# An FFT filter and gated FFN on one core: three of eight batches pass from first to second stage through DRAM, and the second stage runs two iterations later

## The chip, the cores and the metric

The kernel runs on one core of a Trainium2 chip. The metric is the device time of one execution in microseconds, as the median of a few runs. A profiled execution has a span of its own, from its first to its last instruction. The engines of the core are TensorE (PE in the profile; PEld is its weight load), VectorE (DVE), ScalarE (ACT), GpSimd (POOL) and SyncE (SP), which here only issues copies.

## The reference

The input `x` has 8 batches of 3136 rows and 256 columns. Along the rows it is filtered by multiplication in the frequency domain; the result goes through a gated feed-forward block of width 1024.

```python
X = np.fft.rfft(x, axis=1)
y = np.fft.irfft(X * (filt_r + 1j * filt_i)[None], n=3136, axis=1)   # (8, 3136, 256)
h = np.maximum(y @ w_in, 0.0)                                        # (8, 3136, 1024)
conv_out = sum(conv_w[k] * hp[:, k:k + S, :] for k in range(3))      # hp: h padded by one row at each end
out = (h * sigmoid(conv_out)) @ w_out                                # (8, 3136, 256)
```

## The kernel before

**The transform.** 3136 is 112 x 28, and both transforms are done as two small matrix products each. For one batch there are four stages: the first stage (112-point, over `n1`), the second stage (28-point, over `n2`), the product with the filter, the third stage (back over `n2`) and the last stage (back over `n1`). Between the first and the second stage the data has to change places: the first stage has one column block per `n2`, with the 112 rows of (part r, group g) on one axis, and the second stage wants the rows of (n2, r), again 112, for one group g. A batch is cut into 14 pairs p (`NP = 14`), two `n2` in the first stage, two groups in the later ones.

- `first(b, p)` holds the loaded piece of `x` as weights and streams the table `s1_sb` through, so its result comes out with the 256 columns of `x` on the partitions (two blocks of 128). `keep` (L327) copies it with ACT into one of two big tiles `turns[0]`, `turns[1]`, used alternately by batch.
- `turn(b, p)` (L334) transposes four blocks of a finished `turns` tile back with PE against the identity `eye_sb`, which brings the rows (n2, r) of two groups onto the partitions. `turned_rows` (L339) copies that with ACT into a tile named `a` (two buffers).
- `second(b, p)` (L346; L349 for the last pair) multiplies it with `s2_sb` into the PSUM tile `pp` (three buffers).
- `filt(b, p)` makes three products on DVE (L358, L359, L360) and one sum `z` on POOL (L362).
- `third(b, p)` (L233) multiplies `z` with `i1_sb`; `store` (L237, L239) copies the result with ACT and ACT's queue writes it to DRAM as `b_dram`.
- `last_load`, `last_stage` (L215) and `last_out` (L146, L149) read it back and make `y`.

**The order of the first loop.** It is written out by hand: one iteration i handles the pair i-1 in the first stage and, with m = i - SKEW and SKEW = NP + 1 = 15, the pair m in `turn`, m-1 in `second`, m-2 in `filt` and m-4 in `third`; a whole batch must have passed the first stage before its first pair can be turned. On PE the order inside an iteration is third, first, second, turn. The engines PE, ACT, DVE and POOL keep this order; SP's copies are placed by their dependences. `load_first` loads `x` six iterations ahead of its use, into seven buffers; from iteration 10 on `load_filter` brings the filter and the third stage's table, a pair per iteration; from iteration 36 on one step (two in every eighth iteration) of `convert_weights` unpacks the FFN's weights with DVE, ACT and POOL. The steps last until about iteration 106. At iteration `done` = 113 the pools of `x` and the raw weights are closed and `y` gets their place; from then on batch 0 passes the last stage in the place of the first.

**The second loop** runs over 448-row tiles and 128-column blocks of the FFN: `inner` (L177 to L179), `relu`, `conv`, `gate`, `split_g` and `project` (L498 to L500). The last stage of batches 1 to 7 is spread over it.

Of the kernel before, what the change touches and what calls it, by code (L numbers as in the profile page):

```python
# [9 lines left out]
F32 = mybir.dt.float32  # L10
# [3 lines left out]
AF = mybir.ActivationFunctionType  # L14
# [4 lines left out]
N2 = 28  # L19
G = 28  # L20
D = 256
# [103 lines left out]
def tile_fft_filter_gated_ffn(  # L125
# [16 lines left out]
    nc = tc.nc  # L142
    B = x.shape[0]
# [35 lines left out]
        nc.tensor.matmul(ps, lhsT=wl, rhs=rh, start=False, stop=stop, **kw)  # L179

    dram = ctx.enter_context(tc.tile_pool(name="dram", bufs=1, space=bass.MemoryType.DRAM))
    b_dram = [dram.tile([N2, 112, D], F32, name=f"b_dram{b}") for b in range(B)]

    wc = ctx.enter_context(tc.tile_pool(name="wc", bufs=1))
# [24 lines left out]
    def last_stage(b, c, ps):  # L209

        br = lasts[b, c]
        for j in range(2):
            for k in range(KT):
                o = ps[:, (2 * k + j) * N1:(2 * k + j + 1) * N1]
                nc.tensor.matmul(o, lhsT=br[:, j, 128 * k:128 * k + 128], rhs=m2_sb, start=True, stop=True)  # L215
        lasts[b, c] = ps

    def last_out(b, c):
        yh, yl = y_slices(b, slice(c, c + 2))
        pv = lasts.pop((b, c))[:, 0:4 * N1].rearrange("p (k c a) -> p k c a", c=2, a=N1)  # L220
        hi_act(yh, pv)
        lo_dve(yl, pv, yh)

    NP = 14
# [5 lines left out]
    def third(b, p, ps):  # L230
        z = parts.pop((b, p))
        for j in range(2):
            nc.tensor.matmul(ps[:, j], lhsT=i1_sb[:, 2 * p + j], rhs=z[:, j], start=True, stop=True)  # L233

    def store(b, p, ps):
        st = rest.tile([112, 2, D], F32, name="sb")
        nc.scalar.activation(st, ps, AF.Copy)  # L237
        v = b_dram[b].rearrange("n (r g) d -> (n r) g d", g=G)
        nc.scalar.dma_start(out=v[:, 2 * p:2 * p + 2], in_=st)  # L239
# [4 lines left out]
    s1_sb = xp.tile([112, N2, 112], F32, name="s1_sb")  # L244
    with (
# [5 lines left out]
        turns = [pl.tile([128, KT, N2, 112], F32, name=f"turn{k}") for k, pl in enumerate((xp, fc))]  # L251
# [9 lines left out]
        nc.gpsimd.memset(t1_sb[32:64], 0.0)  # L261

        rows = {}

        def load_filter(p):

            sl = slice(2 * p, 2 * p + 2)
            nc.sync.dma_start(out=t2_sb[0:56, sl], in_=fi[0:56, sl])
            nc.sync.dma_start(out=t1_sb[64:120, sl], in_=fr[64:120, sl])
            if p == NP - 1:  # L270
                nc.sync.dma_start(out=t1_sb[0:56, sl], in_=fr[0:56, sl])
            nc.sync.dma_start(out=i1_sb[:, sl], in_=i1[:, sl])
# [44 lines left out]
        def first(b, p):  # L317

            r = rows.pop(("x", b, p))
            ps = fps.tile([128, 512], F32, name="ps")[:, 0:448].rearrange("p (k n m) -> p k n m", k=KT, n=2)  # L320
            for j in range(2):
                for k in range(KT):
                    nc.tensor.matmul(ps[:, k, j], lhsT=r[:, j, 128 * k:128 * k + 128], rhs=s1_sb[:, 2 * p + j], start=True, stop=True)  # L323
            return ps

        def keep(b, p, ps):
            nc.scalar.activation(turns[b % 2][:, :, 2 * p:2 * p + 2], ps, AF.Copy)  # L327

        def turn(b, p):
            ps = fps.tile([112, 2, D], F32, name="ps")  # L330
            for j in range(2):
                for k in range(KT):
                    v = turns[b % 2][:, k].rearrange("p n (r g) -> p (n r) g", g=G)[:, :, 2 * p + j]
                    nc.tensor.transpose(ps[:, j, 128 * k:128 * k + 128], v, eye_sb)  # L334
            return ps

        def turned_rows(b, p, ps):
            r = fp.tile([112, 2, D], F32, name="a", bufs=2)
            nc.scalar.activation(r, ps, AF.Copy)  # L339
            rows["a", b, p] = r  # L340

        def second(b, p):
            r = rows.pop(("a", b, p))
            pp = fps.tile([120, 2, D], F32, name="pp", bufs=3)
            if p < NP - 1:
                nc.tensor.matmul(pp, lhsT=s2_sb, rhs=r, start=True, stop=True)  # L346
            else:
                for j, m in ((0, s2_sb), (1, s2s_sb)):
                    nc.tensor.matmul(pp[:, j], lhsT=m, rhs=r[:, j], start=True, stop=True)  # L349
            psums[b, p] = pp  # L350

        def filt(b, p):


            pp, v = psums.pop((b, p)), turned[p % 2]
            sl = slice(2 * p, 2 * p + 2)
            u = fp.tile([120, 2, D], F32, name="u")
            nc.vector.tensor_mul(u, pp, t1_sb[:, sl])  # L358
            nc.vector.tensor_mul(v[64:120], pp[0:56], t2_sb[0:56, sl])  # L359
            nc.vector.tensor_mul(v[0:56], pp[64:120], t2_sb[64:120, sl])  # L360
            z = rest.tile([120, 2, D], F32, name="z")
            nc.gpsimd.tensor_tensor(out=z, in0=u, in1=v, op=ALU.add)  # L362
            parts[b, p] = z

        def at(i):
            return divmod(i, NP) if 0 <= i < NP * B else None

        XBUFS = 7
        SKEW = NP + 1

        def load_first(i):
            if i < NP and i % 2 == 0:
                nc.sync.dma_start(out=s1_sb[:, 2 * i:2 * i + 4], in_=s1[:, 2 * i:2 * i + 4])
            if bp := at(i):
                load(*bp)
# [2 lines left out]
            load_first(i)  # L378
        csteps, wsteps = convert_conv(), convert_weights()
        done = NP * B + 1  # L380
        NI = done + N2 // 2 + 2
        END = NP * B - 4
        with tc.manual_schedule(engines=COMPUTE):
            for i in range(NI):
                m = i - SKEW
                if i == done:
                    assert next(wsteps, None) is None
                    convert_pools.close()
                    forward_pools.close()
                    yps.append(ctx.enter_context(tc.tile_pool(name="y_even", bufs=1, side="right", reuse_waits="tile")))  # L390
                    lp = ctx.enter_context(tc.tile_pool(name="lp", bufs=2, side="right", reuse_waits="tile"))
                if i:
                    load_first(i + XBUFS - 1)
                if i == 8:
                    nc.sync.dma_start(out=eye_sb, in_=eye)
                    nc.sync.dma_start(out=s2_sb, in_=s2[:, 0:120])
                    raws["cw"] = cv.tile([128, 6 * NF], I32, name="rawc", bufs=1)
                    nc.sync.dma_start(out=raws["cw"], in_=conv_w)
                if 10 <= i < 10 + NP:
                    load_filter(i - 10)  # L400
                if i == 16:
                    nc.sync.dma_start(out=s2s_sb, in_=s2s[:, 0:120])
                    nc.sync.dma_start(out=m2_sb, in_=m2)
                c = 2 * (i - done)
                if 0 <= c - 4 < N2:
                    last_out(0, c - 4)
                if 0 <= c - 2 < N2:
                    last_stage(0, c - 2, fps.tile([128, 512], F32, name="ps"))
                if bp := at(m - 2):
                    filt(*bp)  # L410
                pt = None
                if (bp := at(m - 4)) and m - 4 <= END:
                    pt = fps.tile([112, 2, D], F32, name="ps")
                    third(*bp, pt)
                pf = first(*bp) if (bp := at(i - 1)) else None
                if bp := at(m - 1):
                    second(*bp)
                pa = turn(*bp) if (bp := at(m)) else None
                if pt is not None:
                    store(*at(m - 4), pt)  # L420
                if pf is not None:
                    keep(*at(i - 1), pf)
                if pa is not None:
                    turned_rows(*at(m), pa)
                if 0 <= m - 1 < NP:
                    copy_filter(m - 1)
                if 14 <= i < 22:
                    next(csteps, None)
                if i in (30, 32):
                    load_weights((i - 30) // 2)  # L430
                if i >= 36:
                    for _ in range(2 if i % 8 == 0 else 1):
                        next(wsteps, None)
                if 0 <= c < N2:
                    last_load(0, c)
# [14 lines left out]
    def projected(m):  # L450

        return None if m in PAUSE else at(m - PLAG + sum(m < k for k in PAUSE))

# [67 lines left out]
    for b in range(1, B):  # L521
        start = ((NSUB * (b - 1) - 1) // 2 + 1) * 16 + (4 if b == 1 else 0)
        stop = NSUB * b // 2 * 16 + NSUB * b % 2
# [3 lines left out]
    with tc.manual_schedule(engines=COMPUTE):  # L527
        for m in range(NH + PLAG):
            if m + 4 in pieces:
# [22 lines left out]
                evacuate(*a)  # L552


PLAG = 6
PAUSE = (8,)
AVOID = (3, 4, 5, 6, 7)
# [39 lines left out]
```

## Time and profile before

| | us |
|---|---|
| median of 3 runs (1558.48 to 1562.84) | 1561.46 |
| the profiled execution | 1559.94 |
| its span | 1558.2 |
| PE busy | 1537.8 (99%) |
| DVE busy | 1297.0 (83%) |
| ACT busy | 1245.0 (80%) |
| POOL busy | 703.0 (45%) |
| granted TensorE clock, mean | 0.999 |

The first loop takes about 364 us, the second the rest. In a row of the timeline, the first number is the start in us from the span's start, the second how long it lasts, then engine, line, operation, what is written and read (without buffer numbers), the shape and how many instructions were merged; a bracket gives the idle time just before and what ended it. In a row of a group, the time behind the bar is all of it together, then the mean of one in ns. A line number is one of the kernel before. A matmul in full precision shows as two records, since it passes twice.

### The profile page before, as it was taken

The numbers are of one execution on the slowest core, as the hardware profiler recorded it, in microseconds if no ns is written. First come the engines' busy times: TensorE is split into PE (matmuls) and PEld (weight loads), VectorE is DVE, ScalarE is ACT, GpSimd is POOL, SyncE is SP. The second block draws the span as 40 slices with busy tenths as digits, with TensorE's granted clock in tenths as the row PEclk, the third lists the DMA queues.
The fourth block names the chain that finished last, engine by engine and source line by source line (L and its number), as shares of the span: only waits on it lengthen the run. The fifth ranks groups of instructions, "written<-read, shape, count | busy, mean of one in ns | idle before, by whom it ended". The sixth has DMA issues, their size and how long they took to land.

```text
span 1558.2 us, 27801 instructions
## 1 busy us (share of the span) xinstructions
PE 1537.8 (99%) x10320; PEld 1418.2 (91%) x10320; DVE 1297.0 (83%) x1978; ACT 1245.0 (80%) x2274; POOL 703.0 (45%) x625
## 2 busy tenths in 40 slices
PE   8999999998999999999999999999999999999998
PEld 7787778877999999999999999999999999999998
DVE  3888888788888888888888888888888888888887
ACT  5655555566888888888888888888888888888887
POOL 3455555533444444444444444444444434444444
PEclk9999999999999999999999999999999999999999
DMA  9855555452111011111111011111011110100001
GB/s 236 261 179 168 172 169 164 137 148 78 33 52 48 31 47 48 49 49 47 48 42 36 27 53 52 44 48 48 31 48 42 49 54 27 46 25 25 24 25 48
DMA packets 89062, 115.24 MB, mean 74 GB/s; under 512 B 7400, under 2 KB 60168, under 8 KB 88928
## 3 DMA queue, kind: packets, MB, share of 16 engines
q1 hardware_dynamic: 74592, 87.77, 18.4%
q10 hardware_dynamic: 14336, 25.70, 5.8%
q8 instruction: 82, 1.34, 0.4%
q14 instruction: 52, 0.43, 0.1%
HBM read 62.06 MB, written 51.38 MB: 73 GB/s over the span
## 4 chain that ended last, share of the span: by engine, by line
PE 94%; DMA 2%; DVE 1%; ACT 1%; issue 0%; SPq 0%; POOL 0%; ACTq 0%; POOLq 0%; DVEq 0%
PE ps_h L178 12%; PE ps_h L179 12%; PE ps_h L177 11%; PE po L498 11%; PE po L500 11%; PE po L499 11%; PE ps L233 6%; PE ps_h L215 5%; PE pp L346 5%; PE ps L323 5%; PE ps L334 3%; DMA x<-in_x 1%; PE ps L215 1%; DVE y L149 1%; ACT y L146 0%; PE pp L349 0%
## 5 line engine op out<-in xcount | busy, mean ns | idle before, releaser
L152 POOL TENSOR_TENSOR g<-t,g 128x448 fp32r<-128x448 f32 x448 | 517.1, 1154 | 663.5 <-ACT g L146 259.3
L498 PE MATMUL po<-wo,g 128*128 128x256 f32 x1568 | 441.4, 282 | 0.0
L500 PE MATMUL po<-wo,g 128*128 128x256 f32 x1568 | 433.9, 277 | 0.4 <-POOL g L152 0.4
L499 PE MATMUL po<-wo,g 128*128 128x256 f32 x1568 | 433.4, 276 | 0.0
L472 DVE SCALAR_TENSOR_TENSOR t<-ps_h,cw,t 128x448 f32<-128x448 f32 x448 | 305.7, 682 | 85.6 <-ACT t L467 75.2
L178 PE MATMUL ps_h<-y,wi 128*128 128x450 f32 x896 | 330.3, 369 | 5.6 <-DVE y L149 5.6
L177 PE MATMUL ps_h<-y,wi 128*128 128x450 f32 x896 | 329.1, 367 | 3.3 <-DVE t L478 1.9
L179 PE MATMUL ps_h<-y,wi 128*128 128x450 f32 x896 | 328.8, 367 | 0.0
L473 DVE SCALAR_TENSOR_TENSOR t<-ps_h,cw,t 128x448 f32<-128x448 f32 x448 | 306.5, 684 | 16.0
L467 ACT ACTIVATE t<-ps_h,cw 128x448 f32<-128x448 f32 x448 | 284.8, 636 | 43.2 <-ACT ps_h L465 2.6
L498 PEld LDWEIGHTS po<-wo,g 128*128 128x128 f32 x1568 | 294.8, 188 | 7.1
L499 PEld LDWEIGHTS po<-wo,g 128*128 128x128 f32 x1568 | 294.3, 188 | 5.7
L500 PEld LDWEIGHTS po<-wo,g 128*128 128x128 f32 x1568 | 294.5, 188 | 0.6 <-POOL g L152 0.6
L465 ACT ACTIVATE ps_h<-ps_h 128x450 f32<-128x450 f32 x448 | 251.8, 562 | 32.9 <-PE ps_h L179 27.0
L478 DVE TENSOR_TENSOR t<-ps_h,t 128x448 f32<-128x448 f32 x448 | 275.3, 615 | 0.1
L477 ACT ACTIVATE t<-t 128x448 f32<-128x448 f32 x448 | 255.0, 569 | 12.4 <-DVE t L473 11.2
L146 ACT ACTIVATE g<-t 128x448 fp32r<-128x448 f32 x448 | 254.7, 568 | 0.2 <-DVE t L478 0.2
L362 POOL TENSOR_TENSOR z<-u,v 120x512 f32<-120x512 f32 x112 | 156.6, 1398 | 184.3 <-DVE v L360 154.1
L178 PEld LDWEIGHTS ps_h<-y,wi 128*128 128x128 f32 x896 | 168.3, 188 | 14.7 <-DVE y L149 7.9
L179 PEld LDWEIGHTS ps_h<-y,wi 128*128 128x128 f32 x896 | 168.3, 188 | 13.9
L177 PEld LDWEIGHTS ps_h<-y,wi 128*128 128x128 f32 x896 | 169.9, 190 | 11.7 <-DVE t L478 2.9
L149 DVE TENSOR_TENSOR y<-ps_h,y 128x448 fp32r<-128x448 f32 x98 | 103.1, 1053 | 75.3 <-ACT y L146 75.3
(62 smaller groups left out, 1661.6 us busy)
## 6 DMA issues: line engine op xcount, KB each, us to landing
x<-in_x SPq DMA_DIRECT2D x112, 224.0 KB, 2.9
b_dram<-sb ACTq DMA_DIRECT2D x112, 224.0 KB, 2.3
br<-b_dram SPq DMA_DIRECT2D x112, 224.0 KB, 2.6
out<-ot SPq DMA_DIRECT2D x27, 896.0 KB, 4.1
raw<-in_w_in SPq DMA_DIRECT2D x8, 256.0 KB
raw<-in_w_out SPq DMA_DIRECT2D x8, 256.0 KB
t_sb<-in_fr SPq DMA_DIRECT2D x15, 112.0 KB
t_sb<-in_fi SPq DMA_DIRECT2D x14, 112.0 KB
```

The costliest lines, as they stand in the source:

```text
L152: nc.gpsimd.tensor_tensor(out=dst, in0=src, in1=hi.bitcast(F32), op=ALU.subtract)
L177: nc.tensor.matmul(ps, lhsT=wh, rhs=rh, start=start, stop=False, **kw)
L178: nc.tensor.matmul(ps, lhsT=wh, rhs=rl, start=False, stop=False, **kw)
L179: nc.tensor.matmul(ps, lhsT=wl, rhs=rh, start=False, stop=stop, **kw)
L467: nc.scalar.activation(t, h[:, 1:SUB + 1], AF.Copy, scale=cw[:, 1, f:f + 1])
L472: nc.vector.scalar_tensor_tensor(out=t, in0=h[:, 0:SUB], scalar=cw[:, 0, f:f + 1], in1=t, op0=ALU.mult, op1=ALU.add)
L473: nc.vector.scalar_tensor_tensor(out=t, in0=h[:, 2:SUB + 2], scalar=cw[:, 2, f:f + 1], in1=t, op0=ALU.mult, op1=ALU.add)
L477: nc.scalar.activation(t, t, AF.Sigmoid)
L478: nc.vector.tensor_mul(t, h[:, 1:SUB + 1], t)
L498: nc.tensor.matmul(o, lhsT=gh[:, sl], rhs=wo[0][:, f], start=first, stop=False, skip_group_check=True)
L499: nc.tensor.matmul(o, lhsT=gh[:, sl], rhs=wo[1][:, f], start=False, stop=False, skip_group_check=True)
L500: nc.tensor.matmul(o, lhsT=gl[:, sl], rhs=wo[0][:, f], start=False, stop=last, skip_group_check=True)
```

## The change

Batches 2, 4 and 6 (`THROUGH_DRAM`) take another way from the first to the second stage. Their first stage holds the table `s1_sb` as weights and streams the piece of `x` through (two matmuls of 256 columns in place of four of 112), so its result has (r, g) on the partitions. `keep` copies it into a tile `a` and ACT's queue writes it to a new DRAM tensor `a_dram[b]`. `load_rows` reads two groups of it back with 112 rows (n2, r) on the partitions, on SP's queue, two iterations ahead of the place where `turn` would stand; `second` takes the tile as it is. For these batches there is no `turn`, no `turned_rows` and no `turns` tile; the two tiles alternate over batches 0, 1, 3, 5 and 7. The pool of `a` has four buffers, shared by `keep`, `load_rows` and `turned_rows`. SKEW goes from 15 to 17, so that all stages from the turn on are two iterations later, and so are `load_filter` and the last stage of batch 0 (`LATE` = 2).

```diff
+    a_dram = {b: dram.tile([N2, 112, D], F32, name=f"a_dram{b}") for b in THROUGH_DRAM}
...
+        turned_by = {b: n + 1 for n, b in enumerate(b for b in range(B) if b not in THROUGH_DRAM)}
...
         def first(b, p):
             r = rows.pop(("x", b, p))
+            if b in THROUGH_DRAM:
+                ps = fps.tile([112, 2, D], F32, name="ps")
+                for j in range(2):
+                    nc.tensor.matmul(ps[:, j], lhsT=s1_sb[:, 2 * p + j], rhs=r[:, j], start=True, stop=True)
+                return ps
...
         def keep(b, p, ps):
-            nc.scalar.activation(turns[b % 2][:, :, 2 * p:2 * p + 2], ps, AF.Copy)
+            if b in THROUGH_DRAM:
+                r = fp.tile([112, 2, D], F32, name="a", bufs=ABUFS)
+                nc.scalar.activation(r, ps, AF.Copy)
+                nc.scalar.dma_start(out=a_dram[b][2 * p:2 * p + 2].rearrange("n p d -> p n d"), in_=r)
+            else:
+                nc.scalar.activation(turns[turned_by[b] % 2][:, :, 2 * p:2 * p + 2], ps, AF.Copy)
+
+        def load_rows(b, p):
+            r = fp.tile([112, 2, D], F32, name="a", bufs=ABUFS)
+            v = a_dram[b].rearrange("n (r g) d -> (n r) g d", g=G)
+            nc.sync.dma_start(out=r, in_=v[:, 2 * p:2 * p + 2])
+            rows["a", b, p] = r
...
         def turned_rows(b, p, ps):
-            r = fp.tile([112, 2, D], F32, name="a", bufs=2)
+            r = fp.tile([112, 2, D], F32, name="a", bufs=ABUFS)
...
-        SKEW = NP + 1
+        ABUFS = 4
+        SKEW = NP + 3
+        LATE = SKEW - NP - 1
...
-        NI = done + N2 // 2 + 2
+        NI = done + LATE + N2 // 2 + 2
...
-                if 10 <= i < 10 + NP:
-                    load_filter(i - 10)
+                if 12 <= i < 12 + NP:
+                    load_filter(i - 12)
+                if (bp := at(m + 2)) and bp[0] in THROUGH_DRAM:
+                    load_rows(*bp)
...
-                c = 2 * (i - done)
+                c = 2 * (i - done - LATE)
...
-                pa = turn(*bp) if (bp := at(m)) else None
+                pa = turn(*bp) if (bp := at(m)) and bp[0] not in THROUGH_DRAM else None
...
+THROUGH_DRAM = (2, 4, 6)
```

On PE, where batch 1 ends its second stage and batch 2 begins, there stood before (L233 third stage, L323 first stage, L346 and L349 second stage, L334 turn):

```order
L346 MATMUL pp<-a,s_sb 120x512
L334 MATMUL ps<-eye_sb,turn_98 112x128 x4
L233 MATMUL ps<-z,i_sb 112x256 x2
L323 MATMUL ps<-s_sb,x 128x112 x4
L349 MATMUL pp<-a,s_sb 120x256
L349 MATMUL pp<-a,s2s_sb 120x256
L334 MATMUL ps<-eye_sb,turn_97 112x128 x4
L233 MATMUL ps<-z,i_sb 112x256 x2
L323 MATMUL ps<-s_sb,x 128x112 x4
L346 MATMUL pp<-a,s_sb 120x512
L334 MATMUL ps<-eye_sb,turn_97 112x128 x4
L233 MATMUL ps<-z,i_sb 112x256 x2
```

Each iteration has its four pieces, the turn among them. The same place after (L234 third stage, L330 first stage with `x` as weights, L364 and L367 second stage, L352 turn):

```order
L364 MATMUL pp<-a,s_sb 120x512
L352 MATMUL ps<-eye_sb,turn_100 112x128 x4
L234 MATMUL ps<-z,i_sb 112x256 x2
L330 MATMUL ps<-s_sb,x 128x112 x4
L367 MATMUL pp<-a,s_sb 120x256
L367 MATMUL pp<-a,s2s_sb 120x256
L234 MATMUL ps<-z,i_sb 112x256 x2
L330 MATMUL ps<-s_sb,x 128x112 x4
L364 MATMUL pp<-a,s_sb 120x512
L234 MATMUL ps<-z,i_sb 112x256 x2
L330 MATMUL ps<-s_sb,x 128x112 x4
```

The turn is gone from the iterations that carry batch 2 to the second stage; the order of the others is what it was. On SP, the copies around the first reads of batch 2, before (L314 loads `x`, L285 the raw weights):

```order
L285 DMA raw<-in_w_in 128x512
L285 DMA raw<-in_w_out 128x512
L314 DMA x<-in_x 112x512 x9
L285 DMA raw<-in_w_in 128x512
L285 DMA raw<-in_w_out 128x512
L314 DMA x<-in_x 112x512 x9
```

And after (L316 loads `x`, L287 the raw weights, L344 reads the rows of batch 2 back):

```order
L287 DMA raw<-in_w_in 128x512
L287 DMA raw<-in_w_out 128x512
L316 DMA x<-in_x 112x512 x2
L344 DMA a<-a_dram_57 112x512 x2
L316 DMA x<-in_x 112x512
L344 DMA a<-a_dram_57 112x512
L316 DMA x<-in_x 112x512
L344 DMA a<-a_dram_57 112x512
L316 DMA x<-in_x 112x512
```

The two first reads follow one another; after them each read stands behind one load of `x`, and loads of `x` stand behind reads.

More of the change, by code (lines that the diff above doesn't have):

```diff
@@ L332, in turn @@
                 for k in range(KT):
-                    v = turns[b % 2][:, k].rearrange("p n (r g) -> p (n r) g", g=G)[:, :, 2 * p + j]
+                    v = turns[turned_by[b] % 2][:, k].rearrange("p n (r g) -> p (n r) g", g=G)[:, :, 2 * p + j]
                     nc.tensor.transpose(ps[:, j, 128 * k:128 * k + 128], v, eye_sb)
```

## The prediction

> **What bounds the kernel now.** I read the busy shares first, then the chain of waits, then the busy time by stretches, then TensorE's own timeline. The first line is part 1 of the page, the second its chain.
>
> ```profile
> PE 1537.8 (99%) x10320; PEld 1418.2 (91%) x10320; DVE 1297.0 (83%) x1978; ACT 1245.0 (80%) x2274; POOL 703.0 (45%) x625
> ```
> ```profile
> PE 94%; DMA 2%; DVE 1%; ACT 1%; issue 0%; SPq 0%; POOL 0%; ACTq 0%; POOLq 0%; DVEq 0%
> ```
>
> TensorE (PE) is the bound on average, but a share of 99% can hide a stage with another limit. So the next view cuts the span: columns are the stretch, its length, then busy us (and count) of PE, PEld, DVE, ACT, POOL, the granted clock, the DMA share and GB/s.
>
> ```profile
> 0.00:20.00 20.00, 14.99 (x106) 14.58 (x107) 0.00 (x0) 8.01 (x14) 7.29 (x8) 1.00 0.92 262
> ...
> 100.00:140.00 40.00, 40.00 (x239) 31.95 (x238) 33.81 (x50) 23.92 (x44) 22.88 (x19) 1.00 0.58 174
> ...
> 260.00:300.00 40.00, 40.00 (x238) 31.80 (x238) 32.63 (x50) 23.47 (x43) 23.22 (x17) 1.00 0.50 151
> ```
> ```profile
> 700.00:1500.00 800.00, 797.08 (x5547) 765.65 (x5546) 682.41 (x1055) 694.77 (x1284) 351.12 (x321) 1.00 0.13 41
> ```
>
> From about 60 to 350 us, where the change works, PE has no idle time at all; the start waits for loads; the second loop (from 365 us) is also full, so what the first loop saves reaches the end one for one. This is one steady iteration of the first loop on PE, with the start of each piece:
>
> ```profile
> 297.87 1.03 PE L233 MATMUL ps<-z,i_sb 120*112 120x256 f32 x4
> 298.73 1.04 PE L323 MATMUL ps<-s_sb,x 112*128 112x112 f32 x8
> 299.61 1.03 PE L346 MATMUL pp<-a,s_sb 112*120 112x512 f32 x2
> 300.48 0.60 PE L334 MATMUL ps<-eye_sb,turn 128*112 128x128 f32 x4
> 300.92 1.03 PE L233 MATMUL ps<-z,i_sb 120*112 120x256 f32 x4
> ```
>
> Matmuls overlap, so the second column is no price; the distance between starts is: third stage 0.86, first stage 0.88, second stage 0.87, turn 0.44, sum 3.05 us.
>
> **The turns that go.** Three batches of 14 iterations lose their four transposes: 42 x 0.44 = 18.5 us, on the path. (42 x 4 x the 272 ns mean that the groups give for one transpose would be 45.7 us; that counts the overlap.) The ACT copy that emptied them goes too, off the path.
>
> **First stage with the table stationary.** Four records of 256 columns in place of eight of 112. The trace has no such matmul; the nearest row is the third stage, which also has a 112-column weight tile and 256 columns in four records: 0.86. Against 0.88 that saves 42 x 0.02 = 0.8 us. If it took as much as before the term is 0; I take 0.8.
>
> **VectorE in the shorter iterations.** An iteration without a turn is 0.86 + 0.88 + 0.87 = 2.61 us for PE. VectorE does three products in it and, from iteration 36 to 106, a step of the weight conversion:
>
> ```profile
> 153.16 1.03 PE L346 MATMUL pp<-a,s_sb 112*120 112x512 f32 x2
> ...
> 154.42 0.43 DVE L170 TENSOR_SCALAR em<-ws 128x512 int32<-128x512 int32 x1
> 154.87 0.69 DVE L358 TENSOR_TENSOR u<-pp,t_sb 120x512 f32<-120x512 f32 x1
> 155.58 0.68 DVE L359 TENSOR_TENSOR v<-pp,t_sb 56x512 f32<-56x512 f32 x1
> ...
> 156.29 0.69 DVE L360 TENSOR_TENSOR v<-pp,t_sb 56x512 f32<-56x512 f32 x1
> ...
> 157.02 0.69 DVE L172 SCALAR_TENSOR_TENSOR em<-raw,em 128x512 f32<-128x512 uint32 x1
> ...
> 157.16 1.68 POOL L362 TENSOR_TENSOR z<-u,v 120x512 f32<-120x512 f32 x1 [1.19 <-DVE v L360]
> ...
> 157.74 0.69 DVE L358 TENSOR_TENSOR u<-pp,t_sb 120x512 f32<-120x512 f32 x1
> ...
> 160.56 1.03 PE L233 MATMUL ps<-z,i_sb 120*112 120x256 f32 x4
> ```
>
> From 154.87 to 157.74 is 2.87 us with a long conversion step; the three products alone take 2.15 (154.87 to 157.02). So VectorE becomes the second bound. Its mean load comes from the stretches in which it converts:
>
> ```profile
> 106.00:147.00 41.00, 41.00 (x248) 32.88 (x247) 33.88 (x51) 24.62 (x45) 24.47 (x20) 1.00 0.58 176
> 147.00:190.00 43.00, 43.00 (x257) 34.31 (x257) 37.86 (x55) 24.83 (x44) 24.44 (x18) 1.00 0.58 174
> 190.00:232.00 42.00, 42.00 (x250) 33.38 (x249) 35.05 (x53) 24.92 (x46) 24.39 (x19) 1.00 0.56 167
> 232.00:275.00 43.00, 43.00 (x259) 34.35 (x259) 35.27 (x53) 25.51 (x47) 25.69 (x20) 1.00 0.54 161
> ```
>
> Busy 142.1 us plus 212 gaps of 0.03 (0.72 between starts of 0.69 long) is 148.4 of 169 us, or 2.68 per 3.05 us iteration: 0.07 over the new 2.61. The conversion lasts through 34 of the 42 iterations (14 + 14 + 6), so 34 x 0.07 = 2.4 us come back if every lag reaches PE. The lag first eats slack: the product whose second stage started at 153.16 had its z at 158.84 and was used at 160.56, and of those 1.7 us, 3 x 0.44 go, leaving 0.4. With little to eat I charge the whole 2.4; bounds 0 (slack takes it) and the rival below.
>
> **Two iterations more.** The second stage runs 17, not 15, iterations behind the load. At the start this puts two first stages ahead and the loads of the filter behind two x loads; at the end two iterations (113 and 114) have no first stage and no turn, where before one had no first stage. PE's work is only moved. The one such iteration of before, and the next one's first piece:
>
> ```profile
> 319.22 1.03 PE L233 MATMUL ps<-z,i_sb 120*112 120x256 f32 x4
> 320.09 0.68 PE L349 MATMUL pp<-a,s_sb 112*120 112x256 f32 x2
> ...
> 321.03 0.60 PE L334 MATMUL ps<-eye_sb,turn 128*112 128x128 f32 x4
> 321.47 1.04 PE L215 MATMUL ps<-m_sb,br 112*128 112x112 f32 x8
> ```
>
> Without turn and first stage PE has 0.86 + 0.87 = 1.73 us and VectorE its 2.15: 2 x 0.42 = 0.8 us if no slack covers it (bounds 0 and 0.8); I take 0.8. At the start PE idles 5 of 20 us for loads (first stretch above). The two added first stages take 1.8 us; if their loads come in time nothing is lost, if not up to 1.8. By 20 us loads keep up, so I take 0.3:
>
> ```profile
> 20.00:25.00 5.00, 5.00 (x40) 4.38 (x40) 0.99 (x5) 3.06 (x6) 0.00 (x0) 1.00 0.97 214
> ```
>
> **The copies.** Each of the 42 pairs is written (ACT queue, 1 KB pieces) and read back (SP queue, 2 KB pieces, the same shape as an x load). The landing times of the nearest kinds, for b_dram stores and x loads (us, min/median/max; the x view from 100 to 300 us):
>
> ```profile
> L239 ACTq DMA_DIRECT2D b_dram<-sb x112: 310/311/376, 31.1 to 378.4; - x112
> ...
> DMA to landing us min/median/max: 2.2/2.3/4.2
> ```
> ```profile
> L314 SPq DMA_DIRECT2D x<-in_x x65: 312/312/328, 101.5 to 296.8; - x65
> ...
> DMA to landing us min/median/max: 2.5/2.9/5.8
> ```
>
> A read stands on SP behind an x load that waits for this iteration's first stage, 1.7 us in; the second stage wants it three iterations later at the same place: 7.8 us against at most 5.8. The first pair of a batch also waits for that batch's last write, issued at the end of iteration 14b+14: 4.2 + 5.8 = 10.0 at worst against 3.05 + 3.05 + 2.61 + 1.72 = 10.4. While SP waits there, only x loads queue behind it, six iterations ahead of need. ACT issues 42 more copies of 0.31 us; it is busy 24 of 40 us. All hidden: 0; the price without cover is in the rivals.
>
> Sum: -18.5 - 0.8 + 2.4 + 0.8 + 0.3 = -15.8. The profiled execution took 1559.94 us (span 1558.2), so 1544.1; that execution lies 1.5 below the median of three (1558.48 to 1562.84), which I leave in the range: **1544**.
>
> **Rivals.**
> *VectorE bounds outright (0.19).* In its worst stretch (147 to 190) VectorE needs 37.86 + 55 x 0.03 = 39.5 of 43 us, 2.80 per iteration; 34 x 0.19 = 6.5 in place of 2.4: 1548. Two groups speak for it (after the count: ns min/median/max, then first and last start):
>
> ```profile
> L170 DVE TENSOR_SCALAR em<-ws x8: 426/428/1379, 99.2 to 290.7; 128x512 int32<-128x512 int32 x8
> ```
> ```profile
> L362 POOL TENSOR_TENSOR z<-u,v x112: 1263/1299/1692, 27.1 to 369.4; 120x512 f32<-120x512 f32 x112
> ```
>
> A conversion step of 0.43 has a case of 1.38 and a sum of 1.30 one of 1.69: the two engines hold each other up, and denser work may do it more. Against it: a step mostly starts right behind L360, ahead of POOL. [...]
>
> *The DMA engines fill (0.08).* Sizes by issue (KiB each):
>
> ```profile
> x<-in_x SPq DMA_DIRECT2D x112, 224.0 KB, 2.9
> ...
> raw<-in_w_in SPq DMA_DIRECT2D x8, 256.0 KB
> raw<-in_w_out SPq DMA_DIRECT2D x8, 256.0 KB
> ```
>
> An x load, a row read and a store are 3 x 229 thousand bytes, the weights 59 (4.19 MB over 71 iterations): 747 per 2.61 us, 286 GB/s. Where PE waited for loads (0 to 20 us) they moved 262: 2.85 us per iteration, so only 42 x 0.20 + 0.8 - 1.1 = 8.1 saved: 1552. Against it:
>
> ```profile
> 70.00:75.00 5.00, 5.00 (x32) 3.86 (x31) 3.98 (x7) 2.88 (x5) 3.22 (x3) 1.00 1.03 340
> ```
>
> If copies went one behind another, an iteration would need 2.9 + 2.9 + 2.3 = 8.1 us of them and 42 x (8.1 - 3.05) = 212 us would be lost; but a load and a store, 5.2 us together, already pass in each 3.05 us with PE never idle, so they overlap and I give this no chance. [...]
>
> *Boundary wait (0.04).* If a write and a read each land half again slower than the worst above, 15.0 against 10.4 stops PE for 4.6 us at each of three batches: 13.8 back, 1558, no change.
>
> *ACT stands behind a write (0.03), slower.* In the batches whose first stage goes to DRAM, the "a" buffer that `turned_rows` fills is one that a write of two iterations earlier may still be reading. ACT waits in order, so evictions of all stages queue behind, and PE with them. Cover: 6.1 us. Landing at L costs 42 x (L - 6.1)/2 = 21 (L - 6.1); it eats the 15.8 at L = 6.9, against 4.2 at most for a store now. At L = 7.3 the time is 1569.
>
> **How the numbers follow.** The forecast's own case (0.66) spans 1540.6 (19.3 saved, nothing back) to 1547. With the second case 1548, the runs' spread of 2 us either way and part of the third, the range is 1539 to 1551; it leaves out the last two cases and the worse half of the third. A measurement tells about 0.3%, 5 us, from no change; the first three cases are beyond that, the fourth within, the fifth slower: 0.93, 0.04, 0.03.
>
> **What would show it.** In the new trace, starts of PE pieces 2.61 us apart where batches 2, 4 and 6 pass the second stage and 3.03 to 3.05 elsewhere; the new first stage 0.86; PE idle there caused by L362 or VectorE in the sum of 2 to 3 us; `a` reads landing under 5.8 us with nobody waiting; the second loop of equal length but 16 us earlier. It is wrong if PE's idle time names the row read or ACT, if those iterations are over 2.75 us, or if the DMA share stands at 1.0 there with PE waiting.

## The result and the profile after

| | us |
|---|---|
| before, median of 4 runs (1558.48 to 1562.84) | 1560.82 |
| after, 3 runs (1546.45 to 1546.79) | 1546.70 |
| ratio, 95% interval | 0.991 (0.989 to 0.9929) |
| profiled execution after, its span | 1546.79, 1545.0 |

A fourth run of the changed kernel, with a granted clock of 0.863, took 1670.22 us and is left out. The forecast was 1544.0 with a range of 1539 to 1551. The change made the kernel 14.1 us (0.9%) faster, 2.7 us less than forecast.

Part 1 and the chain of the page after:

```profile
PE 1520.4 (98%) x9984; PEld 1390.8 (90%) x9984; DVE 1295.3 (84%) x1978; ACT 1222.2 (79%) x2232; POOL 704.2 (46%) x625
...
PE 93%; DVE 2%; DMA 2%; ACT 2%; issue 0%; POOL 0%; ACTq 0%; SPq 0%; POOLq 0%; DVEq 0%
```

PE is busy 17.4 us less, which is near what was to go (18.5 + 0.8); the span is only 13.2 us shorter. PE's share fell from 99% to 98%: some of what was saved became waiting. In the new kernel L234 is the third stage, L325 the first stage with the table as weights, L330 with `x` as weights, L337 the write to `a_dram` (ACT's queue), L344 the row read, L357 `turned_rows`, L364 and L367 the second stage, L376 to L378 the three products, L380 the sum on POOL. An iteration in the middle of batch 2's second stage, PE's timeline:

```profile
132.06 1.03 PE L234 MATMUL ps<-z,i_sb 120*112 120x256 f32 x4
132.92 1.04 PE L330 MATMUL ps<-s_sb,x 112*128 112x112 f32 x8
133.80 1.03 PE L364 MATMUL pp<-a,s_sb 112*120 112x512 f32 x2
134.67 1.03 PE L234 MATMUL ps<-z,i_sb 120*112 120x256 f32 x4
```

From start to start of the third stage it is 2.61 us, with the pieces 0.86, 0.88 and 0.87, as worked out. To find what was lost, take the third stage of the same pair of rows in both traces, numbering pairs from 0. Of before:

```profile
55.86 0.81 PE L233 MATMUL ps<-z,i_sb 120*112 120x256 f32 x3
...
81.23 1.03 PE L233 MATMUL ps<-z,i_sb 120*112 120x256 f32 x4
...
105.64 0.81 PE L233 MATMUL ps<-z,i_sb 120*112 120x256 f32 x3
...
361.96 0.81 PE L233 MATMUL ps<-z,i_sb 120*112 120x256 f32 x3
```

And of after (pairs 8, 16, 24, 94 and 108; before's pair 94, at 319.22, stands in the prediction):

```profile
57.52 1.03 PE L234 MATMUL ps<-z,i_sb 120*112 120x256 f32 x4
...
85.82 1.03 PE L234 MATMUL ps<-z,i_sb 120*112 120x256 f32 x4
...
110.09 1.03 PE L234 MATMUL ps<-z,i_sb 120*112 120x256 f32 x4
...
305.85 0.90 PE L234 MATMUL ps<-z,i_sb 120*112 120x256 f32 x3 [0.28 <-POOL z L380]
...
348.59 0.60 PE L234 MATMUL ps<-z,i_sb 120*112 120x256 f32 x2
```

| stretch | before | after | difference | expected from the forecast's gross terms |
|---|---|---|---|---|
| start to pair 8 | 55.86 | 57.52 | +1.66 | +1.76 (two first stages moved here) |
| pair 8 to 16 | 25.37 | 28.30 | +2.93 | -0.16 (8 x 0.02) |
| pair 16 to 24 | 24.41 | 24.27 | -0.14 | -0.1 |
| pair 24 to 94 | 213.58 | 195.76 | -17.82 | -20.8 (42 x 0.44, 28 x 0.02, the two first stages) |
| pair 94 to 108 | 42.74 | 42.74 | 0 | 0 |
| pair 108 to the end | 1196.24 | 1196.41 | +0.17 | 0 |

So there are two losses: 3.1 us between 57 and 86 us, and 3.0 us between pairs 24 and 94, where the shorter iterations lie. The first has this place in the timeline of after:

```profile
74.57 0.60 ACT L336 ACTIVATE a<-ps 112x512 f32<-112x512 f32 x1 [0.60 <-DMA x<-in_x]
...
77.21 0.32 ACTq L337 DMA_DIRECT2D a_dram<-a  x1
...
77.63 0.60 ACT L357 ACTIVATE a<-ps 112x512 f32<-112x512 f32 x1 [2.46 <-DMA x<-in_x]
...
78.28 1.12 PE L364 MATMUL pp<-a,s_sb 112*120 112x512 f32 x2 [1.46 <-ACT a L357]
```

ACT's copy is done at 75.17, and the issue of the write of its result comes at 77.21. For those 2.04 us ACT does nothing, although the turn that L357 is to empty (issued at 74.49, 0.60 long) has been done since 75.1; the profile names the landing of an `x` load as what let it go on. PE then waits 1.46 us for L357. Where nothing holds an issue, it follows the copy by 0.03 us (L336 at 59.98, L337 at 60.61). Both kinds of write were held, up to 2.04 us for `a_dram` and up to 0.64 for `b_dram`, which ACT's queue issues too. In the kernel before no issue of that stretch is held longer than 0.03. In this stretch the DMA engines are full (columns as in the prediction):

```profile
75.00:80.00 5.00, 3.54 (x17) 2.34 (x16) 2.62 (x5) 1.70 (x4) 2.53 (x2) 1.00 1.03 362
```

The second loss, in the timeline of after at iteration 48, where two steps of the weight conversion stand (L166, L168):

```profile
120.61 0.43 DVE L166 TENSOR_SCALAR em<-raw 128x512 int32<-128x512 int32 x1
120.75 1.41 POOL L380 TENSOR_TENSOR z<-u,v 120x512 f32<-120x512 f32 x1 [1.17 <-PE pp L364]
121.07 1.64 DVE L168 SCALAR_TENSOR_TENSOR ws<-em 128x512 f32<-128x512 int32 x1
...
122.75 0.69 DVE L376 TENSOR_TENSOR u<-pp,t_sb 120x512 f32<-120x512 f32 x1
...
126.49 1.12 PE L234 MATMUL ps<-z,i_sb 120*112 120x256 f32 x4 [0.56 <-POOL z L380]
```

The first step starts 0.14 us before POOL's sum. The second meets the sum and takes 1.64 us (0.69 alone); it ends 0.5 us after the sum, which ends at 122.16. The next product waits behind it, and the delay reaches PE one and a half iterations later.

### The profile page after: what moved, and what is told of

Read it like the earlier page. It is cut to its first block, busy times and chain, and to the rows that moved or that the text cites. A ratio compares the mean times of both kernels' runs of the same rounds, so it can differ in the third digit from the quotient of the medians.

```text
span 1545.0 us, 27319 instructions
## 1 busy us (share of the span) xinstructions
PE 1520.4 (98%) x9984; PEld 1390.8 (90%) x9984; DVE 1295.3 (84%) x1978; ACT 1222.2 (79%) x2232; POOL 704.2 (46%) x625
## 4 chain that ended last, share of the span: by engine, by line
PE 93%; DVE 2%; DMA 2%; ACT 2%; issue 0%; POOL 0%; ACTq 0%; SPq 0%; POOLq 0%; DVEq 0%
PE ps_h L178 12%; PE ps_h L179 12%; PE ps_h L177 12%; PE po L520 11%; PE po L522 11%; PE po L521 11%; PE ps_h L216 6%; PE ps L234 5%; PE pp L364 5%; PE ps L330 3%; PE ps L325 2%; PE ps L352 2%; DMA x<-in_x 1%; PE ps L216 1%; DVE y L149 1%; DVE v L378 0%
## 5 line engine op out<-in xcount | busy, mean ns | idle before, releaser
L380 POOL TENSOR_TENSOR z<-u,v 120x512 f32<-120x512 f32 x112 | 157.1, 1403 | 170.9 <-DVE v L378 140.3
```

## The experiments

Before the first of them the theories were these. **Issue:** ACT is held where it issues the write (up to 2.04 us in after), with it L357, which comes next in its order, and PE behind L357 (1.46 us). **Full engines:** between 60 and 85 us the copies are more than the DMA engines can move, and whoever issues, PE waits. **Doubled steps:** VectorE loses time only where two conversion steps fall into a turnless iteration; against it, the prediction's **mean load**, by which every turnless iteration with a conversion step loses 0.07 us.

In the table, "loss" is the time from pair 8 to pair 16 in the profiled run, less 8 x 3.03 us (8 x 3.05 where batch 2 is turned). It is one execution's; the medians are of several.

| kernel | median us (runs) | ratio to before, 95% | loss us |
|---|---|---|---|
| before | 1560.82 | | 0.97 |
| after | 1546.70 | 0.9890 to 0.9929 | 4.06 |
| e2_write_on_sp | 1549.06 (1547.11 to 1550.75) | 0.9907 to 0.9940 | 3.07 |
| e3_batches_3_5_7 | 1546.13 (1544.91 to 1547.42) | 0.9890 to 0.9920 | 0.92 |
| e4_steps_moved | 1543.77 (1541.05 to 1545.96) | 0.9865 to 0.9903 | 4.88 |
| e5_both | 1547.40 (1546.29 to 1548.70) | 0.9899 to 0.9928 | 7.28 |
| e7_weights_later | 1555.24 (1553.18 to 1555.84) | 0.9948 to 0.9974 | 4.31 |
| e8_five_x_buffers | 1545.62 (1543.32 to 1546.17) | 0.9888 to 0.9919 | 2.67 |
| e10_one_iteration_less | 1546.41 (1542.38 to 1549.11) | 0.9889 to 0.9929 | 3.90 |
| e11_batches_4_6 | 1548.61 (1547.17 to 1550.74) | 0.9904 to 0.9940 | 0.57 |
| e18_act_six_a_five_x | 1547.51 (1545.33 to 1548.21) | 0.9902 to 0.9931 | 3.02 |
| e17_3_5_7_one_less | 1547.17 (1546.95 to 1547.32) | 0.9902 to 0.9931 | 1.34 |
| e16_sp_six_a_five_x | 1542.79 (1542.38 to 1543.34) | 0.9872 to 0.9905 | 0.80 |

**The write on SyncE's queue (e2_write_on_sp).**

```diff
-                nc.scalar.dma_start(out=a_dram[b][2 * p:2 * p + 2].rearrange("n p d -> p n d"), in_=r)
+                nc.sync.dma_start(out=a_dram[b][2 * p:2 * p + 2].rearrange("n p d -> p n d"), in_=r)
```

> The changed kernel with one edit: the copy of the first stage's result to DRAM is issued on SyncE's queue, not ScalarE's. Theory: between 63 and 80 us ScalarE stood at its own issue of these copies, waiting for the completion counter of an earlier load, and TensorE lost 4.1 us (four iterations of 3.22 to 4.75 in place of 3.03) behind it. With the issue on SyncE, ScalarE passes by: those iterations come to 3.03 to 3.2, and the time to about 1543 (-3.5 to -4). Rival: the copy engines themselves are full there and TensorE would lose the time in any case: the loss stays within 1 us of 4.1, only another wait is named, 1546 to 1547.

The gain did not come: the loss fell by 1 us, and the median lies above both forecasts. ACT is no longer held at an issue (0.03 us at most from 66 to 80 us), but the timeline of this kernel shows it waiting elsewhere:

```profile
74.94 0.60 ACT L357 ACTIVATE a<-ps 112x512 f32<-112x512 f32 x1 [3.21 <-DMA a_dram<-a]
...
75.59 1.12 PE L364 MATMUL pp<-a,s_sb 112*120 112x512 f32 x2 [2.32 <-ACT a L357]
```

`turned_rows` wants an `a` buffer, and the four are shared with the writes; it gets one when a write to DRAM lands. So the theory of the issue alone fell: taking that wait away uncovered the next.

**Other batches through DRAM (e3_batches_3_5_7).** Batches 3, 5 and 7 in place of 2, 4 and 6, so that the first write comes at iteration 43. The last turn of batch 0 here reads a tile that batch 2 has begun to overwrite; the amount of work is the same.

```diff
-THROUGH_DRAM = (2, 4, 6)
+THROUGH_DRAM = (3, 5, 7)
```

> The changed kernel with batches 3, 5 and 7 in place of 2, 4 and 6 going through DRAM. Theory: the first copies now come at iteration 43, after the loads have caught up, so the 3 to 4 us of the early stall go; but batch 7 passes its second stage beside the last stage of batch 0, where VectorE is busy 17.4 of 18 us, so its 14 missing turns (6.2 us) are worth next to nothing: about 1549. Rival: TensorE bounds the first loop everywhere, so that it does not matter which batches lose their turns: 1543 to 1544.

The early loss is gone, 0.92 us as before the change (0.97). PE's waits between 60 and 90 us, of this kernel (us, times, longest):

```profile
PE ps L234 <- POOL z L380: 0.4, 2, 0.2
```

and of after:

```profile
PE pp L364 <- ACT a L357: 2.5, 3, 1.5
```

The time hardly moved and lies between the two forecasts, because batch 7 is worth little. Its first four iterations without a turn take 2.60 to 2.68 us; the last nine, where its second stage runs beside the last stage of batch 0, take 3.04 to 3.08, as with a turn.

**The doubled steps moved (e4_steps_moved).** The five steps that must be added go to iterations which have a turn.

```diff
-                    for _ in range(2 if i % 8 == 0 else 1):
+                    for _ in range(2 if i in (38, 40, 42, 62, 64) else 1):
```

> The changed kernel with the doubled steps of the weight conversion (every eighth iteration) placed in iterations 38, 40, 42, 62 and 64, all of them with a turn; every other iteration keeps one step. Theory: the 2.6 us that TensorE lost in batches 2 and 4 come from the doubled steps in iterations without a turn, whose second step falls into GpSimd's sum and takes 1.4 to 1.6 us: they go, but for some tenths, and the time is about 1544.3. Rival, the prediction's working by VectorE's mean load: the four or so steps taken out of 34 iterations lower it from 2.68 to 2.64 us each, worth 1 us at most, and the stalls are spread over all of them: 1545.7 or more.

PE's waits from 105 to 350 us, of after and then of this kernel:

```profile
PE ps L234 <- POOL z L380: 1.7, 3, 0.8
```
```profile
PE ps L234 <- POOL z L380: 0.3, 1, 0.3
```

All distances in batch 2's and batch 4's second stage are now 2.59 to 2.62 us, with one conversion step in each, so mean load cost nothing here. The 0.3 that is left is the end of the loop. The median is 2.9 us below that of after; the profiled spans differ by 0.8 only (1544.2 against 1545.0): 2.6 us are saved between pairs 24 and 94, but in this execution pair 8 starts 0.9 us later and the early loss is 0.8 larger. The same step that took 1.64 us now takes 0.69; it starts 0.03 us after the end of the third product (L378, 118.68 to 119.37), for which POOL's sum waits:

```profile
119.40 0.69 DVE L168 SCALAR_TENSOR_TENSOR ws<-em 128x512 f32<-128x512 int32 x1
```

**Both edits (e5_both).** The edits of e2 and e4 together.

> Both edits: the copies on SyncE's queue and the doubled steps moved. Theory: the two losses lie at different places and add up: 1546.7 - 3.7 - 2.4 = about 1540.6. Rival: one loss takes the place of the other (a delay that is cured early comes back later): 1543 or more.

The two did not add up; by the time, the rival held. ACT's group L357, what its engine's idle time waited for:

```profile
  PE ps L352: 34.8, 65
  DMA a_dram<-a: 4.3, 1
```

One wait for one write's landing, 4.3 us, made most of a loss of 7.28. The granted clock then fell as well (third column from the end):

```profile
70.00:75.00 5.00, 2.76 (x13) 1.73 (x11) 3.70 (x6) 0.60 (x1) 3.21 (x3) 1.00 1.04 314
75.00:80.00 5.00, 4.04 (x10) 2.52 (x11) 1.81 (x3) 2.28 (x4) 0.28 (x1) 0.51 0.99 325
80.00:85.00 5.00, 5.00 (x20) 3.72 (x19) 2.06 (x4) 2.28 (x4) 1.27 (x1) 0.81 0.91 289
```

**The weights' loads later (e7_weights_later).** 1 MB of integer weights is loaded at iterations 44 and 46.

```diff
-                if i in (30, 32):
-                    load_weights((i - 30) // 2)
-                if i >= 36:
-                    for _ in range(2 if i % 8 == 0 else 1):
+                if i in (44, 46):
+                    load_weights((i - 44) // 2)
+                if i >= 50:
+                    for _ in range(2 if 60 <= i < 74 or 88 <= i < 93 else 1):
```

> The changed kernel with the doubled conversion steps kept out of the turnless iterations (as in e4_steps_moved, which took 1543.8 us) and, besides, the first two loads of the integer weights (two of 512 KB) moved from iterations 30 and 32 to 44 and 46, behind batch 2's writes; conversion starts at 50 in place of 36. Theory (the copies of 60 to 85 us are more than the 16 DMA engines can move, and ACT or PE stands behind whichever comes last): with 1 MB less in that window, 3 us of transfer at the 300 to 360 GB/s seen there, starts 9 to 14 of the third stage lose under 2 us in place of 4 to 6, and the time is 1541 us (1539.5 to 1542.5). Rival (the catch-up of the x loads alone fills the engines, the weights come behind them in the queue and delay nobody): the loss stays at 4 us or more and the time at 1543.8 us.

On the early loss the rival was right: 4.31 us stay, the weights were not its cause. The time went up for a reason that neither theory had priced: the steps that had to be caught up were doubled in 14 iterations running. From pair 38 to pair 80 this kernel takes 9.5 us more than e4_steps_moved (130.9 against 121.4). Its timeline there:

```profile
174.49 0.69 DVE L164 TENSOR_TENSOR em<-em 128x512 int32<-128x512 int32 x1
174.61 1.71 POOL L380 TENSOR_TENSOR z<-u,v 120x512 f32<-120x512 f32 x1 [2.59 <-DVE v L378]
...
175.22 1.38 DVE L166 TENSOR_SCALAR em<-raw 128x512 int32<-128x512 int32 x1
...
180.63 1.12 PE L234 MATMUL ps<-z,i_sb 120*112 120x256 f32 x4 [0.98 <-POOL z L380]
```

So doubled steps cost in iterations with a turn as well, when they follow one another; spaced, as in e4 and at iterations 40, 64 and 72 of the change, they cost nothing there.

**Five buffers for x (e8_five_x_buffers)**, on e4.

```diff
-        XBUFS = 7
+        XBUFS = 5
```

> As e4_steps_moved, with five buffers for x in place of seven, so that at most five loads of x (224 KB each) are under way and the catch-up after the start is two loads shorter. Theory (the burst of x loads is part of what fills the DMA engines when the first writes to DRAM come): starts 9 to 14 lose 1 to 2 us less, time 1542 us (1541 to 1543). Rival: five buffers are too few in the start, where loads come in at one in 3 us and slower; PE then waits for x itself before 60 us, and the time is 1545 us or more.

The loss is the theory's, the time the rival's. The loss fell from 4.88 to 2.67 in the profiled runs, but the start was 1.1 us later at pair 8 (59.49 against 58.38), and the median is not better than e4's (1545.62 against 1543.77, ranges overlapping). ACT still stood behind a copy between 60 and 85 us:

```profile
ACT a L357 <- DMA x<-in_x: 2.5, 1, 2.5
```

**One iteration less (e10_one_iteration_less)**, on e4.

```diff
-        SKEW = NP + 3
+        SKEW = NP + 2
-                if 12 <= i < 12 + NP:
-                    load_filter(i - 12)
-                if (bp := at(m + 2)) and bp[0] in THROUGH_DRAM:
+                if 11 <= i < 11 + NP:
+                    load_filter(i - 11)
+                if (bp := at(m + 1)) and bp[0] in THROUGH_DRAM:
```

> As e4_steps_moved, with the second stage one iteration later than in the kernel before in place of two, and the rows read back two iterations ahead of their use in place of three; filter loads are issued one iteration earlier to match. Theory (each iteration of delay costs its unfilled part at the start and at the end of the loop, 0.4 us at the end and 0.5 us at the start; the read has time enough, since it lands within 6 us, about 2.3 turnless iterations): 0.4 to 0.9 us less than e4_steps_moved, 1543.1 us, and no wait of PE for a read row. Rival (the first read of each batch waits for the last write of that batch, which is issued one iteration ahead of it: two landings of 2 to 3 us each against 7.7 us): 1 to 3 us of waiting in each of three batches, 1546 to 1549 us.

No gain, and the rival is right for one batch of three: at batch 2's first pair PE waits, and pair 25 takes 4.09 us in place of 2.61. The reads of batch 2 begin at 110.24, 3.60 us after the issue of the last write of that batch at 106.64 (that they wait for its landing is inferred), three of them one behind the other:

```profile
110.24 1.26 SPq L344 DMA_DIRECT2D a<-a_dram  x3
```

PE's timeline has the wait for the first of them:

```profile
115.27 1.09 PE L364 MATMUL pp<-a,s_sb 112*120 112x512 f32 x2 [1.25 <-DVE em L164]
```

The wait is put down to a VectorE step, which does not feed L364; the read does, so that it is the read that PE waits for is inferred. Batches 4 and 6 lost 0.05 and 0. The runs spread over 6.7 us, too wide to read the half microsecond that was looked for.

**Two batches (e11_batches_4_6)**, on e10; the tiles of turns alternate over the other six.

```diff
-THROUGH_DRAM = (2, 4, 6)
+THROUGH_DRAM = (4, 6)
```

> As e10_one_iteration_less, but only batches 4 and 6 go through DRAM; batch 2 is turned by TensorE, so that no copy goes to DRAM before iteration 57 (about 150 us). Theory (batch 2's writes cost about 3 us in the early window, so that batch 2 is worth only 14 x 0.46 = 6.4 less 3 us): e10_one_iteration_less plus 3.5 us, near 1546.7 us, with starts 9 to 14 of the third stage losing 1 us as in the kernel before. Rival (the early loss belongs to the loads and would be there without the writes): e10_one_iteration_less plus 6.4 us, near 1549.5 us.

The loss is 0.57, no more than in the kernel before, which is the theory's and not the rival's. The times can't tell the two apart: this kernel takes 2.2 us more than e10 in the medians and 5.2 more in the profiled spans, and e10's runs spread over 6.7. Here too PE waits for a row read at a batch's start, 0.7 us at batch 4. PE's waits from 60 to 90 us are 0.2 in all, and yet the engines are as full as in the kernel before: share 1.04 and 322 GB/s from 75 to 80 us. So full engines alone did not stop PE here, and none of that wait is for ACT.

```profile
75.00:80.00 5.00, 5.00 (x31) 3.96 (x30) 3.41 (x6) 2.77 (x6) 2.55 (x2) 1.00 1.04 322
```

**Six `a` buffers, five for x, write on SyncE (e16_sp_six_a_five_x) or left on ScalarE (e18_act_six_a_five_x)**, on e4. They differ by one word.

```diff
-        XBUFS = 7
-        ABUFS = 4
+        XBUFS = 5
+        ABUFS = 6
```
```diff
-                nc.scalar.dma_start(out=a_dram[b][2 * p:2 * p + 2].rearrange("n p d -> p n d"), in_=r)
+                nc.sync.dma_start(out=a_dram[b][2 * p:2 * p + 2].rearrange("n p d -> p n d"), in_=r)
```

> As e8_five_x_buffers (steps moved, five buffers for x; 1545.6 us, starts 8 to 15 of the third stage 2.6 us over their 3.03), with the write to DRAM issued on SyncE's queue and six buffers for "a" in place of four. Theory (the copies themselves are not too slow for the program, since the kernel before keeps the engines as full and loses 1 us; what costs is that ScalarE stands behind a copy, first at the issue of a write, and with the write on SyncE at the buffer of a write that has not landed): with both taken away, starts 8 to 15 lose 1 us or less, and the time is 1543 us (1541.5 to 1544.5). Rival (full copy engines delay x or the filter rows as well, whoever issues): 2.5 us or more stay, with PE waiting for x or VectorE for a filter row, 1545.5 us or more.

> As e16_sp_six_a_five_x, but with the write left on ScalarE's queue: six buffers alone. Theory (on its own queue ScalarE is held at the issue of the write, by copies issued before, and not by the buffers): nothing changes against e8_five_x_buffers, 2.5 us stay in starts 8 to 15, 1545.5 us (1544 to 1547). Rival (the four buffers shared by writes, turned rows and reads were short here too): 1 us or less stays, 1543.5 us.

e16 came as the theory said; e18 did in the loss, while its median lies 0.5 us above the theory's range. With both of ACT's waits taken away the loss is 0.80, of which 0.6 is a wait of PE for `x`, which has two buffers fewer. What ACT's group L357 waited for in e16, over the whole loop, is PE alone, and nobody waited for it:

```profile
  PE ps L352: 36.5, 69
```

while the engines move as much as in the kernels that lost:

```profile
70.00:75.00 5.00, 5.00 (x24) 3.50 (x23) 3.18 (x5) 3.61 (x6) 1.92 (x2) 1.00 1.02 333
75.00:80.00 5.00, 5.00 (x26) 3.87 (x25) 3.91 (x6) 2.99 (x5) 1.89 (x2) 1.00 0.98 340
```

With the write on ACT's queue the six buffers help nothing (3.02 against e8's 2.67), and the timeline of e18 is that of after again:

```profile
68.52 0.60 ACT L336 ACTIVATE a<-ps 112x512 f32<-112x512 f32 x1 [0.43 <-ACT sb L238]
...
71.13 0.32 ACTq L337 DMA_DIRECT2D a_dram<-a  x1
...
71.50 0.60 ACT L357 ACTIVATE a<-ps 112x512 f32<-112x512 f32 x1 [2.38 <-PE ps L325]
...
72.15 1.12 PE L364 MATMUL pp<-a,s_sb 112*120 112x512 f32 x2 [1.06 <-ACT a L357]
```

e16 is 3.9 us faster than the changed kernel (1542.38 to 1543.34 against 1546.45 to 1546.79; the two ran on different occasions) and the best version of the study. Seven buffers for `x` with six of `a` were not run.

**Batches 3, 5 and 7 with one iteration less (e17_3_5_7_one_less).** e10 with other batches and the steps doubled at iterations 38 to 46.

```diff
+        SKEW = NP + 2
+THROUGH_DRAM = (3, 5, 7)
+                    for _ in range(2 if i in (38, 40, 42, 44, 46) else 1):
```

> Batches 3, 5 and 7 through DRAM as in e3_batches_3_5_7 (1546.1 us), with the second stage one iteration later than before in place of two, where the tiles of turns are free in time, rows read two iterations ahead, and the doubled conversion steps at iterations 38 to 46. Theory (no write before iteration 43, so starts 8 to 15 lose 1 us as before; batch 7's missing turns are worth little, since VectorE bounds that part beside the second loop's first steps): e3_batches_3_5_7 less 1.1 us for the steps and 0.4 us for the iteration, 1544.6 us. Rival (the first read of a batch waits for its last write, as batch 2's did for 1.5 us in e10_one_iteration_less): up to 1.5 us more in each of three batches, 1546 to 1549 us.

The early loss is small again (1.34), but the time is 2.6 us over the forecast and inside the rival's range. PE's waits from 100 to 365 us hold the reads this time:

```profile
PE ps L234 <- POOL z L380: 1.7, 8, 0.2
PE pp L364 <- DMA a<-a_dram: 1.2, 2, 0.9
```

So two iterations between the read and its use were too few at a batch's boundary here (1.2 us in two waits), in e10 (1.25) and in e11 (0.66); with three, as in the change, nobody waited.

## Why the prediction was right, and where it was off

**The turns: right.** 2.61 us in place of 3.05, in 42 iterations, 18.5 us; with e4's steps every one of the distances shows it.

**The first stage: right.** With the table as weights iterations with a turn take 3.03 in place of 3.05, those without one 2.59 in place of 2.61.

**The copies: this step failed.** It said "All hidden: 0"; it is 3.1 us of the 3.1 + 2.6 + 0.4 that were lost in all. One of the prediction's own signs of being wrong, that PE's idle time names ACT, is there: 2.5 us, though in the stretch of the writes and not in that of the reads, where it was looked for. The step took the landing times of `x` loads from 100 to 300 us, where engines are half idle (share 0.50 to 0.59 in before), and counted an issue as 0.31 us of ACT. But the writes of batch 2 begin at 60 us, where loads still catch up (share 0.92 to 1.03 from 60 to 80 us of after), and there an issue stood for up to 2.04 us. The eviction of a turn that was finished at 75.1 us came at 77.63, behind the issue at 77.21 of a write that nobody was in a hurry for. That it is ACT's place in the order, and not the bandwidth, is shown by e16 and e18, which differ in the queue alone: 0.80 against 3.02 us, and all runs of the one (1543.34 at most) below all of the other (1545.33 at least). The traces fit: PE's longest wait for L357 between 60 and 85 us is 0.99 to 1.67 us wherever batch 2's writes stand on ACT's queue (after, e4, e7, e8, e10, e18), and before, e3, e11 and e16 have none. Of ACT's issues in the rows of that stretch one is held by 2.04 us in after and one by 2.01 in e18, and none by more than 0.03 in before, e2, e5 and e16. The rival "ACT stands behind a write" had the right engine: the mechanism it describes, an `a` buffer held by a write, is what e2 and e5 show, with a longest wait of ACT's L357 of 3.2 and 4.3 us and some shorter ones, and not over 42 pairs. What the profile does not settle is for which earlier copies the issue waits; it names `x` loads, a filter row, a piece of the third stage's table, in e8 weights, and in e18 PE's first stage; e7 shows that the weights need not be among them.

**The DMA engines fill: it happened and cost nothing by itself.** In e16 the share is 0.98 to 1.02 from 70 to 80 us, at 333 to 340 GB/s, and PE is never idle there; in e11 PE is not idle either at 1.04 and 322 GB/s. The rival's 262 GB/s was too low a bound. Its need was well worked out: 286 GB/s where rows are read, against 276 and 271 in after (110 to 150 and 185 to 225 us), at shares of 0.90 and 0.88. It left out the stretch where batch 2's rows are written beside the filter rows, and there the engines filled (1.03 from 75 to 80 us of after).

**VectorE: near in size by luck, wrong in kind.** 2.4 was forecast, 2.6 was lost (the 3.0 of pairs 24 to 94 less 0.4 at the end of the loop). But the forecast spread it as a lag of 0.07 over 34 iterations. The iterations with one conversion step lost 0.2 us in all (pairs 57 and 58), and in e4 nothing. 1.1 us came from iteration 48 and 1.1 from 56, which have no turn and two steps on VectorE; there the second step ran into POOL's sum: 1.64 us in place of 0.69 at 48, 1.38 in place of 0.43 at 56. The doubled iterations 80 and 104, without a turn too, have only one of their steps on VectorE and lost nothing. The 0.3 us at 96, an iteration with a turn, are of another kind: its steps are one on POOL and one on ACT, ACT waited 0.82 us for POOL, and its copy of a turn, L357, came late for PE. A mean load over a stretch hid that. In the rows at 120.75 and 121.07 the step starts 0.32 us after the sum and ends 0.55 us after it (122.71 against 122.16); why the two engines hold each other up is not shown.

**Two iterations more: right in kind, too large.** At the end 0.44 was lost (the two distances are 1.73 and 2.17) where 0.8 was charged: slack took the first lag. At the start, 0.3 was charged and nothing is left at pair 8 (+1.66 against 1.76 of moved work): loads kept up. That is one execution's number: e2, e4, e5 and e7, which do the same up to there, start pair 8 at 57.84 to 58.76 us, 0.3 to 1.2 later than after.

**The boundary: right.** PE waits for no row read in after; with an iteration less, in e10, e11 and e17, it does.

By terms, the forecast was -18.5 - 0.8 + 2.4 + 0.8 + 0.3 + 0 = -15.8, and the trace gives -18.5 - 0.8 + 2.6 + 0.4 - 0.1 + 3.1 = -13.3, against 13.2 between the spans.

## What to carry to other kernels

A copy that was issued from ScalarE's queue stood in ScalarE's order, and at a DMA share of 1.03 its issue was held for 2.04 us and TensorE for 1.46 behind it. So price such a copy by what stands behind it where the DMA engines are full, not by its 0.3 us of issue, and read landing times from the stretch in which it will run. Taking that wait away showed the next (the buffer behind the queue, 3.21 us in e2), and only with both gone was the gain seen (a loss of 0.80 us in e16). Where two engines hold each other up (a step of 0.69 us took 1.64 beside POOL's sum), look at the iterations with the most work on either, not at the mean.

## What was not expected of the hardware

The DMA engines moved 362 GB/s with a share of 1.03 (75 to 80 us of after); the prediction had bounded them by the 262 GB/s of the start, and its highest row was 340. After a longer stop of PE in e5 (2.76 of 5 us busy) the granted clock was 0.51 in the next 5 us and 0.81 in the 5 after those. That wait cost more than its length: from the start of L364 behind it (75.96) to that of the next L364 (82.00) it is 6.04 us, with no wait of PE named between, and from there to the one after (85.03) 3.03. In after's early stretch, with 3.54 of 5 us busy at worst, it stayed at 1.00. Where the first loop ends, PE waits 3.3 us in after, and the clock of the 5 us behind it (355 to 360) is 0.68; the kernel before has 0.78 from 365 to 370, and from pair 108 to the end the two differ by 0.17 us only. The idle time of PE that the profile names at the drop in e5 is 2.96 us; what makes the clock fall is not shown:

```profile
75.96 2.06 PE L364 MATMUL pp<-a,s_sb 112*120 112x512 f32 x2 [2.96 <-ACT a L357]
```

The runs of one kernel on one chip spread differently: 6.7 us for e10, 4.9 for e4, 1.0 for e16, 0.4 for e17. No run shows why; the start, which varies by 1.2 us at pair 8 (above), is a part of it. Where the spread is 5 us, a change of 2 cannot be read from one execution.
